# Crossbar transfers of q issued one block sooner in a pooled-attention and MLP kernel

## The chip, the cores and the metric

The kernel runs on one core of one Trainium2 chip. The time is device microseconds of one execution on that core; a lower time is better. Timed runs are given by their median. The profile is one further execution, recorded by the hardware profiler.

## The reference

The inputs q, k and v have the shape 8 batches x 8 heads x 576 rows x 64. Per batch and head, k and v are averaged over groups of 8 rows (72 groups), the scores are taken against the 72 pooled keys, and the softmax of them weighs the 72 pooled values. A residual MLP follows, first over the 576 rows, then over the 512 channels.

```
k_p = k.reshape(B, H, 72, 8, D).mean(axis=3);  v_p likewise
attn = softmax(q @ k_p.T / sqrt(D));  x = (attn @ v_p) -> (B, 576, 512)
u = x + lam * einsum('ts,bsd->btd', w_tok, alpha1 * x + beta1)
out = u + lam * (relu((alpha2 * u + beta2) @ w_ch1) @ w_ch2)     # 512 -> 2048 -> 512
```

All data is float32 in memory; the kernel's matmuls take bf16 and f16.

## The kernel before

The output is cut into 36 chunks of 128 rows, and four chunks make a block, so there are nine blocks n = 0 to 8. Block n runs the channel MLP of its four chunks: 16 steps `mlp_A` (L471; hidden columns, ReLU on ScalarE) and 16 steps `mlp_B` (L487; back to 512 channels, added on VectorE, stored by SP). Woven into it is the attention of batch b = n + 1 and the row mixing that makes the chunks of later blocks. Blocks 7 and 8 have no attention left.

Inside a block the order is written out by hand: a list of pairs (slot, step), sorted by slot (L620 to L648). Slots 0 to 15 hold the 16 steps of `mlp_A`, 16 to 31 those of `mlp_B`; a negative slot comes first in its block. A slot is only a sort key: each engine and each queue takes its own instructions in this order, and waits only for what they need. A step far down the list can therefore run early, on an engine that has nothing in front of it.

The steps that matter here, for one batch b > 1:

- The first 512 rows of q are loaded by GpSimd, two DMAs `q_bf` that turn float32 into bf16 (L79). The raw k and the last 64 rows of q and k (`load_rem`, L91: four DMAs) are loaded by SP, as is v (`load_v`, L101: two DMAs for each half).
- `cast_rem` (L112) casts the last rows of q to bf16 on GpSimd (L116) and sums those of k (L118). `sum_k` (L127) makes the first sums over k on GpSimd (L131, L133).
- `att_F` (L305) turns q so that the head dimension lies on the partitions: a crossbar transfer (DMA transpose) on the SP queue, `qT`, two for a batch (L314). `att_Frem` (its transfer at L332) does the same for the last rows, `rem_qT`, one for a batch. For batches 0 and 1 both go through TensorE.
- `att_K` (from L342) pools k by small matmuls (L348, L351) and VectorE copies the result into `kpT` (L356). `att_V` (from L358) pools v on VectorE. `att_S` multiplies `kpT` with `qT` (L374), then with `rem_qT` (L377), and ScalarE takes the exponential. `att_AV` follows (L393, L397).
- `mix_T` and `mix_uT` make the rows of later blocks; the latter is a crossbar transfer `u_fm` on the SP queue (L456).

In the slots of block n, with b = n + 1 and b > 1: `cast_rem(b)` at -2.0, both `att_F(b)` at -1.1, `sum_k(b)` at -0.9 and 0.3, `att_Frem(b)` at 0.2, `att_V(b)` from 0.2 to 6.2, the v loads of batch b + 1 at 3.5 and 7.5, `att_K(b)` at 4.1 and 6.1, `att_S(b)` from 7.4 on, the stores of the four output chunks at 19, 23, 27 and 31, `mix_uT` from 20.9 on, and the loads of q and k of batch b + 1 at 21.0 and 21.2 with `load_rem(b + 1)` at 21.1. Nothing on GpSimd stands between `sum_k(b)` and those loads of q.

Of the kernel before, what the change touches and what calls it, by code (L numbers as in the profile page):

```python
# [9 lines left out]
BF = mybir.dt.bfloat16  # L10
# [4 lines left out]
P = 128  # L15
# [8 lines left out]
def kernel(  # L24
# [18 lines left out]
    nc = tc.nc  # L43
    ctx.enter_context(tc.manual_schedule())
    B, H, S, D = q.shape

    const = ctx.enter_context(tc.tile_pool(name="const", bufs=1))
    work = ctx.enter_context(tc.tile_pool(name="work", bufs=1))
# [3 lines left out]
    def gp(name):  # L52
        return psA.tile([P, 512], FP, tag="gp", name=name)
# [11 lines left out]
    st1 = {}  # L65

    def new_batch(b):
        st1[b] = {"qT": [None] * 2, "ET": [None] * H, "raw": [None] * 2, "q_raw": [None] * 2, "q": [None] * 2,
                  "k": [None] * 2, "v": [None] * 2}

    def load_qk(b, u, behind=None):

        def rows(src):
            return src[b, 4 * u:4 * u + 4, 0:512, :].rearrange("h (p c) d -> p h (c d)", c=4)

        raw = work.tile([P, 4, 4, D], FP, tag="k_raw", bufs=2, name="k_raw")
        if b > 1:
            bf = work.tile([P, 4, 4, D], BF, tag="q_bf", bufs=4, name="q_bf")
            nc.gpsimd.dma_start(out=bf.rearrange("p h c d -> p h (c d)"), in_=rows(q))  # L79
            st1[b]["q"][u] = bf  # L80
        else:
            q_raw = work.tile([P, 4, 4, D], FP, tag="q_raw", bufs=2, name="q_raw")
            if behind is not None:
                behind.memset(q_raw[:, 0, 0, 0:1], 0.0)
                behind.memset(raw[:, 0, 0, 0:1], 0.0)
            nc.sync.dma_start(out=q_raw.rearrange("p h c d -> p h (c d)"), in_=rows(q))
            st1[b]["q_raw"][u] = q_raw
        nc.sync.dma_start(out=raw.rearrange("p h c d -> p h (c d)"), in_=rows(k))
        st1[b]["raw"][u] = raw

    def load_rem(b, queue=nc.sync):  # L91

        raw = work.tile([P, 2, 2, 2, D], FP, tag="rem_raw", bufs=2, name="rem_raw")
        for i, src in enumerate((q, k)):
            for h in range(2):
                queue.dma_start(
                    out=raw[:, i, h].rearrange("p c d -> p (c d)"),
                    in_=src[b, h::2, 512:576, :].rearrange("a (i c) d -> i a (c d)", c=2))
        st1[b]["rem_raw"] = raw
# [12 lines left out]
    def cast_rem(b, eng, copy=None):  # L112
        raw = st1[b]["rem_raw"]
        rq = work.tile([P, 2, 2, D], BF, tag="rem_q", bufs=2, name="rem_q")
        rk = work.tile([P, 2, 2, D], BF, tag="rem_k", bufs=2, name="rem_k")
        (copy or eng.tensor_copy)(out=rq.rearrange("p c h d -> p h c d"), in_=raw[:, 0])  # L116
        twice = [raw[:, 1, :, c].unsqueeze(2).to_broadcast((P, 2, 2, D)) for c in range(2)]
        eng.tensor_tensor(out=rk, in0=twice[0], in1=twice[1], op=ALU.add)  # L118
        st1[b]["rem"] = rq, rk

    def cast_q(b, u, copy):

        bf = work.tile([P, 4, 4, D], BF, tag="q_bf", bufs=4, name="q_bf")
        copy(out=bf, in_=st1[b]["q_raw"][u])
        st1[b]["q"][u] = bf
# [40 lines left out]
    for i, src in ((1, moe_alpha1), (0, moe_lam)):  # L166
        n = 65 if i in (0, 3) else 1
        nc.gpsimd.dma_start(out=vecs[0:n:64, i],
                            in_=src.unsqueeze(0).to_broadcast((1 + n // 65, DM)))
# [135 lines left out]
    def att_F(b, hp):  # L305


        st = st1[b]
        u, r = hp // 2, hp % 2
        if r == 0:  # L310
            st["qT"][u] = work.tile([P, 8, P], BF, tag="qT", bufs=4, name="qT")
        if b > 1:
            if r == 0:
                nc.sync.dma_start_transpose(out=st["qT"][u],  # L314
                                            in_=st["q"][u].rearrange("p h c d -> p (h c d)"))
            return
        ps_q = gp("ps_q").bitcast(BF)
        for c in range(4):
            nc.tensor.transpose(
                out=ps_q[:, 128 * c:128 * c + 128],  # L320
                in_=st["q"][u][:, 2 * r + c // 2, 2 * (c % 2):2 * (c % 2) + 2].rearrange(
                    "p c d -> p (c d)"),
                identity=identity_bf)
        nc.scalar.copy(out=st["qT"][u][:, 4 * r:4 * r + 4, :],
                       in_=ps_q[:, 0:512].rearrange("p (c t) -> p c t", c=4))

    def att_Frem(b, copy=None):

        st = st1[b]
        st["rem_qT"] = work.tile([P, 2, P], BF, tag="rem_qT", bufs=2, name="rem_qT")  # L330
        if copy is None:
            nc.sync.dma_start_transpose(out=st["rem_qT"],  # L332
                                        in_=st["rem"][0].rearrange("p c h d -> p (c h d)"))
            return
        ps_q = gp("ps_qr").bitcast(BF)
        for c in range(2):
            nc.tensor.transpose(out=ps_q[:, 128 * c:128 * c + 128],
                                in_=st["rem"][0][:, c].rearrange("p h d -> p (h d)"),
                                identity=identity_bf)
        copy(out=st["rem_qT"], in_=ps_q[:, 0:256].rearrange("p (c t) -> p c t", c=2))  # L340
# [244 lines left out]
    def attention(b):  # L585


        late = b == 1
        todo = [(11.9 if late else -2.0, lambda: cast_rem(b, nc.gpsimd)),
                (14.4 if late else 0.2, lambda: att_Frem(b, nc.scalar.copy if late else None))]  # L590
        for u in range(2):
            at = 10.0 + 4.8 * u if late else -1.0 + 1.2 * u
            if late:
                todo.append((at, lambda u=u: cast_q(b, u, nc.gpsimd.tensor_copy)))
            todo.append((at + 0.1, lambda u=u: sum_k(b, u, nc.gpsimd)))
            for r in range(2):
                at = 12.7 + 4.6 * u + 1.6 * r
                hp = 2 * u + r
                todo.append((at if late else -1.1, lambda hp=hp: att_F(b, hp)))
                todo.append((at + 0.5 if late else 0.2 + 2.0 * hp, lambda hp=hp: att_V(b, hp)))  # L600
                if r:
                    todo.append((at + 0.4 if late else 4.1 + 2.0 * u,
                                 lambda u=u: att_K(b, u, nc.vector.tensor_copy)))
        for h in range(8):
            at = 17.0 + 0.9 * h if late else 7.4 + 1.15 * h
            lag = 1.6 if late else 2.0
            todo.append((at, lambda h=h: att_S(b, h)))
            todo.append((at + lag, lambda h=h: att_AV(b, h)))
            if h % 2:
                eng = nc.gpsimd if late and h < 5 else nc.vector  # L610
                todo.append((at + lag + 0.1, lambda h=h, eng=eng: att_X(b, h - 1, h + 1, eng)))
        for c in range(5):
            at = 26.2 + 0.9 * c if late else 19.1 + 1.3 * c
            todo.append((at, lambda c=c: mix_T(b, c)))
            if c < 4 or b % 2:
                key = (b, c) if c < 4 else (b - 1, 4)
                todo.append((at + 1.8, lambda key=key: mix_uT(key)))
        return todo

    for n in range(NBLK):  # L620
        todo = []
        for j in range(0 if n else 4, NJ):
            todo.append((j, lambda j=j: mlp_A(n, j)))
        for m in range(4):
            for part in range(4):
                at = 16 + (4 * m + part if n else 4 * part + m)
                todo.append((at, lambda m=m, part=part: mlp_B(n, m, part)))
        if n == 0:
            todo.append((11.4, lambda: mix_T(0, 4)))
            todo.append((10.8, lambda: (setup_wtok(4, nc.scalar.copy), setup_rowsum(4))))  # L630
            todo.append((13.3, setup_wtok_odd))
            for g in range(1, 4):
                todo.append((4 * g - 0.8, lambda g=g: setup_bias(g)))
            for g in range(4):
                todo.append((4.2 + 1.7 * g, lambda g=g: scale_w2(g)))
        b = n + 1
        if b < B:
            todo += attention(b)
            if b + 1 < B:
                new_batch(b + 1)  # L640
                for u in range(2):
                    at = 20.0 + 0.2 * u if b == 1 else 21.0 + 0.2 * u
                    todo.append((at, lambda b=b, u=u: load_qk(b + 1, u)))
                    at = 22.0 + 0.2 * u if b == 1 else 3.5 + 4.0 * u
                    todo.append((at, lambda b=b, u=u: load_v(b + 1, u)))
                todo.append((20.1 if b == 1 else 21.1, lambda b=b: load_rem(b + 1)))
        for _, do in sorted(todo, key=lambda x: x[0]):
            do()  # L648

# [29 lines left out]
```

## Time and profile before

| | |
|---|---|
| median of 3 runs | 387.51 us (385.63 to 389.5) |
| profiled execution, its time | 388.71 us |
| profiled execution, span from first to last instruction | 387.0 us |
| TensorE (PE) busy | 356.9 us, 92% |
| VectorE (DVE) busy | 229.0 us, 59% |
| ScalarE (ACT) busy | 158.3 us, 41% |
| GpSimd (POOL) busy | 83.4 us, 22% |
| mean granted TensorE clock | 0.976 of 2.4 GHz |

The rows that are quoted further down give the start in us from the first instruction, then the duration in us. PE is TensorE's matmul, PEld its weight load, SPq the queue of SyncE (its rows are the issuing of DMAs, not the transfers). What stands in square brackets is the idle time of the engine ahead of the instruction and what ended it. In the rows by stretch each engine has its busy time with its number of instructions, and behind them come the granted TensorE clock as a share of full speed, the busy share of the DMA engines and the rate they moved.

### The profile page before, as it was taken

What the parts mean: (1) busy time and instruction counts of PE and PEld (TensorE: products, weight loads), DVE (VectorE), ACT (ScalarE), POOL (GpSimd) and SP (SyncE); (2) the same over time, 40 slices, a digit from 0 to 9 for tenths busy, and PEclk for the clock granted to TensorE, in tenths of its full rate; (3) what the DMA queues carried; (4) which work ended last, traced back from release to release, by engine and by line L of the source; (5) the groups of instructions that cost most, each with busy time, mean ns of one, the idle gap of its engine ahead of it and who ended that gap; (6) DMA issues with size and microseconds to landing.
All of it is one profiled execution on the core that took longest, in us unless ns stands there. A gap on an engine that the chain in (4) does not pass through costs nothing.

```text
span 387.0 us, 5796 instructions
## 1 busy us (share of the span) xinstructions
PE 356.9 (92%) x2179; PEld 190.6 (49%) x2179; DVE 229.0 (59%) x459; ACT 158.3 (41%) x317; POOL 83.4 (22%) x94
## 2 busy tenths in 40 slices
PE   2789998799999799979999799969999999999994
PEld 1375655345644464445545454536445644544542
DVE  4796749788775768484776487546748773011011
ACT  2574766127900690067304650348007701722810
POOL 7653143930007000620043002600060000000000
PEclk9999999899999999998999899979999999999999
DMA  8999996656327952895088806792273024002011
GB/s 200 223 192 214 253 219 145 111 102 165 81 79 195 158 109 64 213 168 107 27 219 128 164 2 186 157 165 45 66 208 90 0 56 118 4 29 81 2 52 57
DMA packets 63931, 46.93 MB, mean 121 GB/s; under 512 B 31448, under 2 KB 54044, under 8 KB 63904
## 3 DMA queue, kind: packets, MB, share of 16 engines
q1 hardware_dynamic: 54496, 38.55, 41.8%
q0 software_dynamic: 9408, 8.02, 14.1%
q8 instruction: 17, 0.28, 0.3%
q14 instruction: 10, 0.08, 0.1%
HBM read 38.04 MB, written 9.44 MB: 123 GB/s over the span
## 4 chain that ended last, share of the span: by engine, by line
PE 80%; DMA 11%; DVE 4%; issue 1%; ACT 1%; SPq 1%; POOL 1%; POOLq 0%; DVEq 0%
PE ps_ch L495 30%; PE ps_h L477 29%; PE ps_tok L442 11%; PE ps_sc L374 4%; DMA rem_qT<-rem_q 3%; DMA v_u<-in_v_dram 3%; DMA rem_raw<-in_q_dram 3%; PE ps_av L393 2%; DMA vecs<-in_moe_beta_dram 2%; PE ps_sc L377 1%; DVE xs L408 1%; DVE v_u L362 1%; PE ps_w L247 1%; DVE x_tm L401 1%; PE ps_bc L229 1%
## 5 line engine op out<-in xcount | busy, mean ns | idle before, releaser
L482 ACT ACTIVATE Hj<-ps_h,bias_cols 128x512 bf16<-128x512 f32 x144 | 98.5, 688 | 161.5 <-PE ps_h L477 160.5
L477 PE MATMUL ps_h<-u_fm,w 128*128 128x512 bf16 (+2 forms) x592 | 141.9, 383 | 0.0
L495 PE MATMUL ps_ch<-w,Hj 128*128 128x512 bf16 x576 | 135.3, 380 | 0.0
L477 PEld LDWEIGHTS <-w 128*128 128x128 bf16 x592 | 63.2, 115 | 51.4 <-issue 8.0
L495 PEld LDWEIGHTS <-Hj 128*128 128x128 bf16 x576 | 55.3, 98 | 62.4 <-issue 1.1
L500 DVE TENSOR_TENSOR u_sb<-u_sb,ps_ch 128x512 f32<-128x512 f32 x36 | 24.7, 687 | 73.0 <-PE ps_ch L495 72.6
L442 PE MATMUL ps_tok<-xs,wtT 128*128 128x512 bf16 (+1 forms) x200 | 50.8, 387 | 2.7 <-DVE xs L408 2.7
L379 ACT ACTIVATE ET<-ps_sc 72x256 f16<-72x256 f32 (+1 forms) x128 | 45.0, 403 | 14.0 <-PE ps_sc L374 9.0
L444 DVE TENSOR_TENSOR u_sb<-x_tm,ps_tok 128x512 f32<-128x512 f32 (+1 forms) x40 | 27.5, 687 | 25.6 <-PE ps_tok L442 24.0
L116 POOL CAST rem_q<-rem_raw 128x256 bf16<-128x256 f32 x7 | 4.5, 646 | 167.9 <-DMA rem_raw<-in_q_dram 167.8
L362 DVE TENSOR_TENSOR v_u<-v_u 72x512 f32<-72x512 f32 x64 | 37.3, 583 | 2.0 <-DMA v_u<-in_v_dram 0.4
L374 PE MATMUL ps_sc<-qT,kpT 128*72 128x256 bf16 x128 | 27.6, 300 | 8.9 <-DMA qT<-q_bf 4.5
L401 DVE TENSOR_TENSOR x_tm<-ps_av,rec 128x320 f32<-128x320 f32 x64 | 31.4, 491 | 2.3
L442 PEld LDWEIGHTS <-wtT 128*128 128x128 bf16 (+1 forms) x200 | 19.4, 99 | 26.4 <-issue 5.0
L399 DVE RECIPROCAL rec<-ps_av 128x5 f32<-128x5 f32 x64 | 12.2, 191 | 31.7 <-PE ps_av L397 30.8
L446 DVE TENSOR_TENSOR u_bf<-u_sb,al_bc 128x512 bf16<-128x512 f32 (+1 forms) x38 | 29.3, 771 | 1.5
L393 PEld LDWEIGHTS <-ET 72*128 72x128 f16 x256 | 16.7, 102 | 12.6 <-ACT ET L379 1.0
L408 DVE TENSOR_TENSOR xs<-x_tm,lamal_bc 128x512 bf16<-128x512 f32 x29 | 22.0, 758 | 0.9
L131 POOL TENSOR_TENSOR k_raw<-k_raw 128x512 f32<-128x512 f32 x16 | 21.2, 1326 | 4.9 <-DMA k_raw<-in_k_dram 4.9
L133 POOL TENSOR_TENSOR k_bf<-k_raw 128x512 bf16<-128x512 f32 x16 | 21.7, 1358 | 1.3
L374 PEld LDWEIGHTS <-kpT 128*72 128x72 bf16 x128 | 12.5, 123 | 15.7 <-DVE v_u L362 4.8
L393 PE MATMUL ps_av<-vp,ET 72*128 72x66 f16 x256 | 18.7, 200 | 0.4 <-ACT ET L379 0.4
(98 smaller groups left out, 208.8 us busy)
## 6 DMA issues: line engine op xcount, KB each, us to landing
k_raw<-in_k_dram SPq DMA_DIRECT2D x16, 512.0 KB
v_u<-in_v_dram SPq DMA_DIRECT2D x16, 512.0 KB
out_dram<-u_sb SPq DMA_DIRECT2D x32, 256.0 KB
w<-in_moe_w_ch_dram POOLq DMA_DIRECT2D x8, 512.0 KB, 14.1
q_bf<-in_q_dram POOLq DMA_DIRECT2D x12, 256.0 KB, 5.7
q_raw<-in_q_dram SPq DMA_DIRECT2D x4, 512.0 KB
rem_raw<-in_q_dram SPq DMA_DIRECT2D x16, 64.0 KB
rem_raw<-in_k_dram SPq DMA_DIRECT2D x16, 64.0 KB
```

The lines of the kernel that those rows point to most:

```text
L362: nc.vector.tensor_tensor(out=t[:, :, 0:n], in0=t[:, :, 0:n], in1=t[:, :, n:2 * n], op=ALU.add)
L374: nc.tensor.matmul(out=ps_sc[0:SPG, 0:256], lhsT=kpT_pool[u][:, half, h % 4, :], rhs=st["qT"][u][:, 2 * (h % 4):2 * (h % 4) + 2, :])
L379: nc.scalar.activation(out=ET[:, n0:n0 + n], in_=ps_sc[0:SPG, 0:n], func=AF.Exp, bias=0.0, scale=0.125)
L393: nc.tensor.matmul(out=av[:, c, :], lhsT=ET[:, m0:m0 + 128], rhs=vp1[:, hh, :])
L401: nc.vector.tensor_tensor(out=x[:, :, dd:dd + D], in0=av[:, :, 0:64], in1=rec.unsqueeze(2).to_broadcast((P, 5, D)), op=ALU.mult)
L408: eng.tensor_tensor(out=xs[:, 0:4, cols], in0=x[:, 0:4, cols], in1=lamal_bc[:, cols].unsqueeze(1).to_broadcast((P, 4, D * (h1 - h0))), op= ...
L442: nc.tensor.matmul(out=ps_tok, lhsT=wtT[0:kk, at, t0:t0 + P], rhs=xs[0:kk, sc, :], start=(sc == 0), stop=(sc == 4))
L444: nc.vector.tensor_tensor(out=s["u"][p0:p1, :], in0=st1[b]["x"][p0:p1, c, :], in1=ps_tok[p0:p1, 0:DM], op=ALU.add)
L446: eng.tensor_tensor(out=s["u_bf"][p0:p1, :], in0=s["u"][p0:p1, :], in1=al2_bc[p0:p1, :], op=ALU.mult)
L477: nc.tensor.matmul(out=ps_h[:, t0:t1], lhsT=w1_of(cc, j), rhs=u_fm[n][:, cc, t0:t1], start=(cc == 0), stop=(cc == 3))
L482: nc.scalar.activation(out=t, in_=ps_h, func=AF.Relu, bias=bias_cols[:, j:j + 1], scale=1.0)
L495: nc.tensor.matmul(out=ps, lhsT=Hj[n, j][:, 128 * m:128 * m + 128], rhs=w2[j // 4][:, j % 4, :], start=(j == 0), stop=(j == NJ - 1))
```

## The change

For batches 3 to 7 the two transfers `qT` move from slot -1.1 of the block that uses them to slots 10.0 and 10.1 of the block before, and `cast_rem` with `att_Frem` from -2.0 and 0.2 to 27.4 and 27.5 of the block before. The loads `q_bf` of the next batch become a step of their own, at slots 0.4 and 0.5 in place of 21.0 and 21.2, and `load_rem` goes from 21.1 to 20.9, which sorts it ahead of the first `mix_uT` (19.1 + 1.8 is just above 20.9 in floating point). Batch 2 keeps the old places of its transfers; its q loads stay in block 0. Nothing is computed in another way.

```diff
--- before.py
+++ after.py
@@ -68,24 +68,26 @@
         st1[b] = {"qT": [None] * 2, "ET": [None] * H, "raw": [None] * 2, "q_raw": [None] * 2, "q": [None] * 2,
                   "k": [None] * 2, "v": [None] * 2}
 
+    def rows(src, b, u):
+        return src[b, 4 * u:4 * u + 4, 0:512, :].rearrange("h (p c) d -> p h (c d)", c=4)
+
+    def load_q_bf(b, u):
+
+        bf = work.tile([P, 4, 4, D], BF, tag="q_bf", bufs=4, name="q_bf")
+        nc.gpsimd.dma_start(out=bf.rearrange("p h c d -> p h (c d)"), in_=rows(q, b, u))
+        st1[b]["q"][u] = bf
+
     def load_qk(b, u, behind=None):
 
-        def rows(src):
-            return src[b, 4 * u:4 * u + 4, 0:512, :].rearrange("h (p c) d -> p h (c d)", c=4)
-
         raw = work.tile([P, 4, 4, D], FP, tag="k_raw", bufs=2, name="k_raw")
-        if b > 1:
-            bf = work.tile([P, 4, 4, D], BF, tag="q_bf", bufs=4, name="q_bf")
-            nc.gpsimd.dma_start(out=bf.rearrange("p h c d -> p h (c d)"), in_=rows(q))
-            st1[b]["q"][u] = bf
-        else:
+        if b < 2:
             q_raw = work.tile([P, 4, 4, D], FP, tag="q_raw", bufs=2, name="q_raw")
             if behind is not None:
                 behind.memset(q_raw[:, 0, 0, 0:1], 0.0)
                 behind.memset(raw[:, 0, 0, 0:1], 0.0)
-            nc.sync.dma_start(out=q_raw.rearrange("p h c d -> p h (c d)"), in_=rows(q))
+            nc.sync.dma_start(out=q_raw.rearrange("p h c d -> p h (c d)"), in_=rows(q, b, u))
             st1[b]["q_raw"][u] = q_raw
-        nc.sync.dma_start(out=raw.rearrange("p h c d -> p h (c d)"), in_=rows(k))
+        nc.sync.dma_start(out=raw.rearrange("p h c d -> p h (c d)"), in_=rows(k, b, u))
         st1[b]["raw"][u] = raw
 
     def load_rem(b, queue=nc.sync):
@@ -586,8 +588,17 @@
 
 
         late = b == 1
-        todo = [(11.9 if late else -2.0, lambda: cast_rem(b, nc.gpsimd)),
-                (14.4 if late else 0.2, lambda: att_Frem(b, nc.scalar.copy if late else None))]
+        todo = []
+        if late:
+            todo = [(11.9, lambda: cast_rem(b, nc.gpsimd)),
+                    (14.4, lambda: att_Frem(b, nc.scalar.copy))]
+        if b == 2:
+            todo = [(-2.0, lambda: cast_rem(b, nc.gpsimd)), (0.2, lambda: att_Frem(b))]
+        if 1 < b < B - 1:
+            todo.append((10.0, lambda: att_F(b + 1, 0)))
+            todo.append((10.1, lambda: att_F(b + 1, 2)))
+            todo.append((27.4, lambda: cast_rem(b + 1, nc.gpsimd)))
+            todo.append((27.5, lambda: att_Frem(b + 1)))
         for u in range(2):
             at = 10.0 + 4.8 * u if late else -1.0 + 1.2 * u
             if late:
@@ -596,7 +607,8 @@
             for r in range(2):
                 at = 12.7 + 4.6 * u + 1.6 * r
                 hp = 2 * u + r
-                todo.append((at if late else -1.1, lambda hp=hp: att_F(b, hp)))
+                if b < 3:
+                    todo.append((at if late else -1.1, lambda hp=hp: att_F(b, hp)))
                 todo.append((at + 0.5 if late else 0.2 + 2.0 * hp, lambda hp=hp: att_V(b, hp)))
                 if r:
                     todo.append((at + 0.4 if late else 4.1 + 2.0 * u,
@@ -641,9 +653,11 @@
                 for u in range(2):
                     at = 20.0 + 0.2 * u if b == 1 else 21.0 + 0.2 * u
                     todo.append((at, lambda b=b, u=u: load_qk(b + 1, u)))
+                    todo.append((at if b == 1 else 0.4 + 0.1 * u,
+                                 lambda b=b, u=u: load_q_bf(b + 1, u)))
                     at = 22.0 + 0.2 * u if b == 1 else 3.5 + 4.0 * u
                     todo.append((at, lambda b=b, u=u: load_v(b + 1, u)))
-                todo.append((20.1 if b == 1 else 21.1, lambda b=b: load_rem(b + 1)))
+                todo.append((20.1 if b == 1 else 20.9, lambda b=b: load_rem(b + 1)))
         for _, do in sorted(todo, key=lambda x: x[0]):
             do()
 
```

## Rows read from the trace of the kernel before

**Rows 1.** Page, chain that ended last: shares of the span by line.

```profile
PE ps_ch L495 30%; PE ps_h L477 29%; PE ps_tok L442 11%; PE ps_sc L374 4%; DMA rem_qT<-rem_q 3%; DMA v_u<-in_v_dram 3%; DMA rem_raw<-in_q_dram 3%; PE ps_av L393 2%; DMA vecs<-in_moe_beta_dram 2%; PE ps_sc L377 1%; DVE xs L408 1%; DVE v_u L362 1%; PE ps_w L247 1%; DVE x_tm L401 1%; PE ps_bc L229 1%
```

**Rows 2.** Busy time by stretch, one row for each of blocks 1 to 6.

```profile
87.94:124.99 37.05, 37.05 (x230) 19.81 (x229) 26.43 (x54) 15.98 (x33) 6.82 (x7) 1.00 0.55 134
124.99:164.34 39.35, 37.38 (x230) 19.73 (x229) 26.50 (x54) 15.73 (x32) 7.64 (x8) 1.00 0.63 132
164.34:205.69 41.35, 38.80 (x231) 20.08 (x229) 26.52 (x54) 15.84 (x32) 9.24 (x10) 0.96 0.61 130
205.69:246.54 40.85, 38.90 (x230) 20.13 (x229) 26.99 (x54) 15.84 (x32) 8.24 (x9) 0.96 0.61 128
246.54:289.70 43.16, 39.95 (x231) 20.52 (x229) 25.78 (x54) 15.84 (x32) 7.53 (x8) 0.92 0.61 123
289.70:326.76 37.06, 37.06 (x231) 19.82 (x229) 26.21 (x54) 15.40 (x32) 0.49 (x1) 1.00 0.26 63
```

**Rows 3.** Waits of the whole span at the scores: us in total, times, longest.

```profile
PE ps_sc L374 <- DMA qT<-q_bf: 4.5, 3, 2.0
...
PE ps_sc L377 <- DMA rem_qT<-rem_q: 3.3, 4, 1.2
...
PE ps_sc L374 <- DVE v_u L362: 1.9, 1, 1.9
```

**Rows 4.** TensorE in order of time: blocks 5 and 6.

```profile
252.60 0.28 PE L348 MATMUL ps_kp<-pool_main,k_bf 128*128 128x64 bf16 x4
...
255.76 0.38 PE L374 MATMUL ps_sc<-qT,kpT 128*72 128x256 bf16 x2 [1.96 <-DMA qT<-q_bf]
257.39 0.24 PE L377 MATMUL ps_sc<-rem_qT,kpT 128*72 128x64 bf16 x1 [1.25 <-DMA rem_qT<-rem_q]
...
296.80 0.38 PE L374 MATMUL ps_sc<-qT,kpT 128*72 128x256 bf16 x2
```

**Rows 5.** Busy time by stretch, the 10 us around block 5's first scores.

```profile
253.80:263.80 10.00, 6.79 (x35) 3.58 (x35) 2.74 (x8) 4.25 (x10) 0.00 (x0) 0.66 0.92 166
```

**Rows 6.** SP queue in order of time: starts of blocks 1, 3, 5, 6.

```profile
89.00 2.75 SPq L314 DMA_TRANSPOSE qT<-q_bf  x2
...
165.52 4.44 SPq L314 DMA_TRANSPOSE qT<-q_bf  x2
...
245.06 2.60 SPq L502 DMA_DIRECT2D out_dram<-u_sb  x2
247.77 5.99 SPq L314 DMA_TRANSPOSE qT<-q_bf  x2
254.23 1.17 SPq L332 DMA_TRANSPOSE rem_qT<-rem_q  x1
255.50 2.55 SPq L108 DMA_DIRECT2D v_u<-in_v_dram  x4
274.68 0.37 SPq L502 DMA_DIRECT2D out_dram<-u_sb  x1
...
290.88 2.66 SPq L314 DMA_TRANSPOSE qT<-q_bf  x2
```

**Rows 7.** GpSimd in order of time, around the start of block 5.

```profile
239.50 0.76 POOL L116 CAST rem_q<-rem_raw 128x256 bf16<-128x256 f32 x1 [32.45 <-DMA rem_raw<-in_q_dram]
...
245.16 1.26 POOL L133 TENSOR_TENSOR k_bf<-k_raw 128x512 bf16<-128x512 f32 x1
246.37 1.53 POOL L79 DMA_DIRECT2D q_bf<-in_q_dram  x2
```

**Rows 8.** The instructions of tile q_bf: its loads, issue to landing.

```profile
DMA to landing us min/median/max: 4.3/5.7/7.9
```

**Rows 9.** Chain of waits in order of time, block 3.

```profile
170.07 4.43 DMA rem_qT<-rem_q
```

**Rows 10.** VectorE in order of time: blocks 3 and 5.

```profile
168.86 0.94 DVE L356 CAST kpT<-ps_kp 64x288 bf16<-64x288 f32 x2 [1.03 <-PE ps_kp L351]
...
255.64 0.29 DVE L364 TENSOR_TENSOR vp<-v_u 72x128 f16<-72x128 f32 x1
```

## The prediction

> **What bounds the kernel now.** I read first the chain that ended last. Three TensorE lines, the two MLP halves and the row mixing, hold 70% of the span; two of the DMA entries, at 3% each, are transfers for q's last rows, `rem_qT` and the load of their raw data [rows 1]. So TensorE sets the end and the question is where it stands still or runs slowly.
>
> The busy time by block answers that. Blocks 1 to 6 have the same TensorE work, 230 or 231 matmuls each, but blocks 1 and 6 take 37.05 and 37.06 us with TensorE busy all the time at full clock, while blocks 2 to 5 take 39.35, 41.35, 40.85 and 43.16 us [rows 2]. Over 37.05 that is 2.30 + 4.30 + 3.80 + 6.11 = 16.51 us. It has two parts. TensorE is idle for span less busy time: 1.97 + 2.55 + 1.95 + 3.21 = 9.68 us. And its busy time is longer than 37.05 by 0.33 + 1.75 + 1.85 + 2.90 = 6.83 us, with a mean granted clock of 0.96, 0.96 and 0.92 in blocks 3 to 5 and 1.00 in block 2 [rows 2].
>
> The waits name the idle part: 4.5 us on `qT` in three blocks, 3.3 us on `rem_qT` in four, and 1.9 us once put down to VectorE: 9.7 us in all, the whole 9.68 [rows 3]. Block 5 shows the place: TensorE idles 1.96 us ahead of the first scores until `qT` lands and 1.25 us more until `rem_qT` lands, while in block 6 the same scores start 7.10 us after the block's start with no wait [rows 4]. The 10 us around block 5's stall have a granted clock of 0.66 [rows 5], a mix of the levels 1.2 and 2.4 GHz: the clock fell after the idle time, and the matmuls behind it ran slowly. So the second part comes out of the first.
>
> The 1.9 us belong to `qT` too, as I read it. It is block 3's wait, where the first scores need `kpT`'s first half; VectorE had that ready at 168.86 + 0.94 = 169.80 [rows 10], and block 3's `rem_qT` transfer, which SP issues behind both `qT`, ran from 170.07 for 4.43 us [rows 9], to 174.50, well after the scores could have begun at 164.34 + 7.10 = 171.44.
>
> Why is `qT` late? On the SP queue both transfers stand behind the previous block's last stores. In block 5 they start at 247.77, 1.2 us into the block, and SP needs 5.99 us to issue the two; block 3's pair takes 4.44. In blocks 1 and 6 the same two take 2.75 and 2.66 us [rows 6]. What differs is GpSimd: in block 5 it issues both q loads of the next batch at 246.37, just as SP comes to the transfers [rows 7]; block 6 has no next batch, and block 1's loads were issued in block 0. Those loads take 4.3 to 7.9 us to land [rows 8].
>
> **The change, part by part.** All times are those of block 5, the worst one, unless said.
>
> *The two `qT`* leave the block's start. Removed from the path: the first wait of each of blocks 2 to 5, 4.5 + 1.9 = 6.4 us [rows 3]. Their new place is behind the v loads of the block before. SP ends those at 255.50 + 2.55 = 258.05 and next has something to do at 274.68 [rows 6], 16.6 us later, or 10.5 us once the block is 6.11 us shorter. The loads they need were issued by 246.37 + 1.53 = 247.90 and land within 7.9 us [rows 7, 8], at 255.8, so SP doesn't stand there for them. No row shows `qT` behind v loads; I bound it by the rows with and without a load beside it, 2.66 and 5.99 us, and take 5.99, since v is then still in flight. Either end fits into the 10.5 us, and the result is needed most of a block later: cost 0. Without that cover each further us would push the store at slot 19 and then the loads of k.
>
> *`cast_rem` and `att_Frem`* leave the block's start as well: removed, the four second waits, 3.3 us [rows 3]. In time the cast hardly moves: it already ran at 239.50, as soon as its data came, 32.45 us after GpSimd had nothing else to do [rows 7]. On SP the transfer now stands between the stores of chunks 2 and 3; the first of these two began at 245.06 and one store takes 0.37 to issue [rows 6], so it goes out at about 245.5. The same transfer at 254.23 released TensorE at 257.39, 3.16 us later [rows 4, 6], and block 3's took 4.43 [rows 9]. By the longer it lands at 250, and a TensorE without stalls wants it at about 246.54 + 7.10 + 0.2 = 253.8. Cost 0, cover 3.8 us. Its issue of 1.17 us [rows 6] delays only the store of chunk 3 and the v loads, which nobody waits for within the block.
>
> *The q loads* go from slot 21 to 0.4, but GpSimd already issues them when `k_bf` ends, at 246.37 against 245.16 + 1.26 = 246.42 [rows 7]; nothing of its own stood between. Same place, cost 0.
>
> *`load_rem`* goes ahead of the first `mix_uT` and the k loads. Four issues like it take SP 2.55 us (the v loads, rows 6), so the first k load may come up to 2.55 us later; the second stands behind the same work as before. The k sums ended at 246.42 and the second half's are first used at 252.60 [rows 4, 7]: 6.2 us of cover. Cost 0.
>
> *The clock.* With the stalls gone nothing is left that slows it: in blocks 1 and 6, which have no stall, it is 1.00 throughout [rows 2]. The bounds of what goes: 9.7 us, if only the waits went, and 16.5 us, if these blocks become like 1 and 6. I take 16.5, because those two blocks have the same matmuls and the same VectorE chain, and differ in just this point. More can't be gained: a block without idle time at full clock is 37.05 us.
>
> The sum is 388.71 - 16.51 = 372.2 us for the profiled execution. That execution is 1.20 us above the median of 387.51, so against the median I say **371.0 us**.
>
> **Rivals.**
>
> *A. The last rows stay late.* `att_Frem` meets the loads again: it goes out at about 245.5 and GpSimd's loads at 246.37 [rows 7], while k sums that end earlier would bring those loads forward too. If its transfer then takes over twice the 4.43 us, the 3.3 us of second waits [rows 3] remain, with none to all of the 6.83 us of slow matmuls: 374.3 to 381.1. For it speaks that `qT` took twice as long beside these loads [rows 6]; against it, that the transfer alone, beside the same loads, never took over 4.43. The Trainium skill (DMA: Bandwidth & Descriptors, section on queues, rings and completion order) says that each DMA engine goes round between the queues that have work, a packet of each at a time. By that rule being issued ahead of the loads buys only the head start and no precedence, which is this rival; the trace agrees so far as the slower `qT` show it.
>
> *B. The same wait under another name.* If block 3's 1.9 us really were VectorE's, and the k and v chain on VectorE were as late as `qT` in all four blocks, the scores would start no sooner: 386 to 388. Against it: `kpT` was ready at 169.80, and block 6 has that chain and starts on time [rows 4, 10].
>
> *C. Slower: SP is held at slot 10.* `qT` now stands ahead of the stores, of `mix_uT` and of the loads of k on an in-order queue. Should the two transfers hold SP for long, the k loads come late and TensorE waits at the k matmuls of the next block (252.60 in block 5). It takes 10.5 us to use up SP's idle time and 6.2 us more to use up the k sums' cover. From 16.7 us on each us costs one in each of blocks 2 to 6, and from 20 us on the 16.5 us gained are lost; at 21 us it is 371.0 + 5 x 4.3 = 392.5. The longest pair so far took 5.99.
>
> **How the numbers follow.** About 1% is what a measurement of this kernel can tell from no change: the three runs lie within 0.5% of their median. Forecast 0.74; A 0.14; B 0.08; C 0.04. The forecast spreads by the runs' own 2 us downwards, to 369, and upwards to the lower bound of the gain, 387.5 - 9.7 = 377.8. The range 369 to 378 holds nearly all of the forecast and the cheaper half of A, near 0.8. Faster by over 1% (under 383.6): the forecast and A, 0.88. Within 1%: B, 0.08. Slower: C, 0.04.
>
> **What the changed profile would show.** Right: blocks 2 to 5 at 37 to 38 us each with a clock of 1.00, no wait at the first scores, `rem_qT` gone from the chain, the pairs of `qT` on SP about 11 us into the block before, and SP idle again before the first store. A would show as waits on `rem_qT` of 0.6 us and more in the scores; B as waits of the scores on VectorE; C as waits of the k matmuls on GpSimd. Wrong above all would be any block among 2 to 5 that still takes 39 us, or blocks without idle time that are longer than 37.05 us.

## The result and the profile after

The changed kernel takes 372.22 us (median of 4 runs, 370.7 to 372.95) against 387.85 us before (4 runs): a ratio of 0.9595, 95% interval 0.9538 to 0.9653. The forecast was 371.0, range 369 to 378. The profiled execution takes 372.95 us with a span of 371.2 us; 372.2 was forecast for it.

The busy time by block (blocks 1 to 6, columns as in [rows 2]; some matmul records are missing, 225 to 227 of 230 are there):

```profile
88.70:125.73 37.03, 36.76 (x225) 19.81 (x229) 26.38 (x54) 15.98 (x33) 6.63 (x7) 1.00 0.64 150
125.73:162.80 37.07, 36.86 (x227) 19.83 (x229) 26.21 (x54) 15.40 (x32) 7.28 (x8) 1.00 0.68 143
162.80:199.85 37.05, 36.84 (x226) 19.80 (x229) 26.18 (x54) 15.40 (x32) 9.60 (x11) 1.00 0.71 143
199.85:236.90 37.05, 36.78 (x225) 19.83 (x229) 26.45 (x54) 15.40 (x32) 8.02 (x8) 1.00 0.66 144
236.90:273.95 37.05, 36.84 (x226) 19.81 (x229) 26.16 (x54) 15.40 (x32) 7.34 (x8) 1.00 0.68 141
273.95:311.00 37.05, 36.78 (x225) 19.79 (x229) 26.22 (x54) 15.40 (x32) 0.00 (x0) 1.00 0.18 47
```

All six blocks are 37.03 to 37.07 us with the clock at 1.00. Blocks 2 to 5 fall from 164.71 us [rows 2] to 148.22 us: 16.49 us, where 16.51 was forecast. The span fell by 15.8 us; the difference lies ahead of block 1, which starts at 88.70 here and at 87.94 before. No instruction of that stretch was changed, and the starts of block 1 in this and the experiments' profiles are spread from 85.3 to 88.7. In this profile and in that of before the granted clock is 0.50 (1.2 GHz) for some of block 0, at 77 to 79 us here and at 76 to 78 before; in the second and the third experiment's, where block 1 starts at 85.3 and 85.9, it stays at 1.00 from 60 us on.

The scores of block 5 on TensorE, which answer to [rows 4]:

```profile
244.00 0.38 PE L376 MATMUL ps_sc<-qT,kpT 128*72 128x256 bf16 x2
244.22 0.24 PE L379 MATMUL ps_sc<-rem_qT,kpT 128*72 128x64 bf16 x1
```

They start 7.10 us into the block, as in block 6 before, and wait for nothing. The SP queue of block 5 and GpSimd around it, which answer to [rows 6, 7]:

```profile
234.72 1.19 SPq L334 DMA_TRANSPOSE rem_qT<-rem_q  x1
...
240.41 7.11 SPq L110 DMA_DIRECT2D v_u<-in_v_dram  x4
247.62 4.07 SPq L316 DMA_TRANSPOSE qT<-q_bf  x2
258.91 0.37 SPq L504 DMA_DIRECT2D out_dram<-u_sb  x1
...
271.69 1.19 SPq L334 DMA_TRANSPOSE rem_qT<-rem_q  x1
```

```profile
236.18 1.53 POOL L77 DMA_DIRECT2D q_bf<-in_q_dram  x2
...
267.56 1.26 POOL L133 TENSOR_TENSOR k_raw<-k_raw 128x512 f32<-128x512 f32 x1 [3.05 <-DMA k_raw<-in_k_dram]
...
271.80 1.27 POOL L135 TENSOR_TENSOR k_bf<-k_raw 128x512 bf16<-128x512 f32 x1
```

The pair `qT` now goes out 10.7 us into the block before its use, takes 4.07 us and is done 7.2 us before SP's next store. `rem_qT` goes out 2.2 us ahead of block 5 and 1.5 us ahead of GpSimd's loads; over blocks 2 to 5 it is 1.2 to 2.3 us ahead of the block and 1.3 to 2.0 us ahead of the loads. GpSimd issues these loads at the block's start, as ever.

### The profile page after: what moved, and what is told of

Same layout as the page of the kernel before. It is cut to its first block, busy times and chain, and to the rows that moved or that the text cites. A ratio compares the mean times of both kernels' runs of the same rounds, so it can differ in the third digit from the quotient of the medians.

```text
span 371.2 us, 5743 instructions
## 1 busy us (share of the span) xinstructions
PE 347.1 (93%) x2139; PEld 188.5 (51%) x2179; DVE 226.5 (61%) x459; ACT 156.7 (42%) x317; POOL 83.0 (22%) x94
## 4 chain that ended last, share of the span: by engine, by line
PE 80%; DMA 8%; DVE 8%; issue 2%; POOL 1%; SPq 0%; POOLq 0%; DVEq 0%
PE ps_ch L497 32%; PE ps_h L479 30%; PE ps_tok L444 11%; DMA v_u<-in_v_dram 3%; PE ps_sc L376 3%; DMA rem_raw<-in_q_dram 3%; DVE v_u L364 2%; DMA vecs<-in_moe_beta_dram 2%; PE ps_av L395 2%; DVE x_tm L403 2%; DVE xs L410 1%; PE ps_sc L379 1%; DVE vp L366 1%; DVE rec L401 1%; DVE xs L519 0%
## 5 line engine op out<-in xcount | busy, mean ns | idle before, releaser
L479 PE MATMUL ps_h<-u_fm,w 128*128 128x512 bf16 (+2 forms) x571 | 136.1, 374 | 1.1
L444 PE MATMUL ps_tok<-xs,wtT 128*128 128x512 bf16 (+1 forms) x195 | 49.7, 384 | 3.7 <-DVE xs L410 3.5
L446 DVE TENSOR_TENSOR u_sb<-x_tm,ps_tok 128x512 f32<-128x512 f32 (+1 forms) x40 | 27.5, 688 | 24.8 <-PE ps_tok L444 24.2
L364 DVE TENSOR_TENSOR v_u<-v_u 72x512 f32<-72x512 f32 x64 | 36.3, 567 | 4.8 <-DMA v_u<-in_v_dram 3.3
L118 POOL CAST rem_q<-rem_raw 128x256 bf16<-128x256 f32 x7 | 3.0, 429 | 132.2 <-DMA rem_raw<-in_q_dram 132.2
L376 PE MATMUL ps_sc<-qT,kpT 128*72 128x256 bf16 x128 | 26.7, 291 | 3.1 <-DVE x_tm L403 1.8
L395 PEld LDWEIGHTS <-ET 72*128 72x128 f16 x256 | 16.5, 102 | 12.2 <-DVE v_u L364 0.8
L358 DVE CAST kpT<-ps_kp 64x288 bf16<-64x288 f32 x28 | 12.7, 455 | 7.7 <-PE ps_kp L353 7.3
```

Source lines behind the costliest of these rows:

```text
L364: nc.vector.tensor_tensor(out=t[:, :, 0:n], in0=t[:, :, 0:n], in1=t[:, :, n:2 * n], op=ALU.add)
L376: nc.tensor.matmul(out=ps_sc[0:SPG, 0:256], lhsT=kpT_pool[u][:, half, h % 4, :], rhs=st["qT"][u][:, 2 * (h % 4):2 * (h % 4) + 2, :])
L395: nc.tensor.matmul(out=av[:, c, :], lhsT=ET[:, m0:m0 + 128], rhs=vp1[:, hh, :])
L444: nc.tensor.matmul(out=ps_tok, lhsT=wtT[0:kk, at, t0:t0 + P], rhs=xs[0:kk, sc, :], start=(sc == 0), stop=(sc == 4))
L446: nc.vector.tensor_tensor(out=s["u"][p0:p1, :], in0=st1[b]["x"][p0:p1, c, :], in1=ps_tok[p0:p1, 0:DM], op=ALU.add)
L479: nc.tensor.matmul(out=ps_h[:, t0:t1], lhsT=w1_of(cc, j), rhs=u_fm[n][:, cc, t0:t1], start=(cc == 0), stop=(cc == 3))
```

## The experiments

The theory to test was that TensorE waits because SP needs 4.4 to 6 us for a pair of `qT` beside GpSimd's q loads. Its rivals: the last rows are late on their own account; or the place behind the last stores makes `qT` late, whatever runs beside it.

**Only the two `qT` moved.**

```diff
-        if b == 2:
+        if b >= 2:
             todo = [(-2.0, lambda: cast_rem(b, nc.gpsimd)), (0.2, lambda: att_Frem(b))]
...
-            todo.append((27.4, lambda: cast_rem(b + 1, nc.gpsimd)))
-            todo.append((27.5, lambda: att_Frem(b + 1)))
```

> The change with the cast and the transfer of q's last rows put back to slots -2.0 and 0.2; only the two qT stay moved. Theory (the stalls come from SP taking 4.4 to 6 us for the two qT beside GpSimd's q loads): with them gone SP reaches rem_qT some 1.2 us into the block instead of 6 to 8, it lands by 6 us, TensorE wants it 7.3 us in: no wait, 372 to 373 us, the whole gain. Rival (the last rows are late on their own account, beside the q loads): waits of 0.6 us and more on rem_qT stay in blocks 2 to 5, with slow matmuls behind them: 375 to 380 us.

Measured: 374.12 us, ratio 0.9651 (0.9564 to 0.9738). Four of blocks 1 to 5 take 37.05 to 37.10 us, block 3 takes 38.41. Its busy time, its rows on TensorE, GpSimd's loads, and its chain of waits:

```profile
161.87:200.28 38.41, 37.20 (x230) 19.80 (x229) 26.04 (x54) 15.62 (x32) 9.26 (x11) 1.00 0.69 137
```

```profile
168.97 0.38 PE L376 MATMUL ps_sc<-qT,kpT 128*72 128x256 bf16 x2
170.56 0.24 PE L379 MATMUL ps_sc<-rem_qT,kpT 128*72 128x64 bf16 x1 [1.21 <-DMA rem_qT<-rem_q]
```

```profile
162.01 1.54 POOL L77 DMA_DIRECT2D q_bf<-in_q_dram  x2
```

```profile
163.06 7.46 DMA rem_qT<-rem_q
```

The theory holds in three of the four blocks; in one the last rows' transfer, issued 1.05 us after the loads, took 7.46 us beside them, where it had 6.1 (out 1.2 us into the block, wanted at 7.3). So the two `qT` bring nearly all of the gain (block 3 loses 1.36 us, and the intervals of this ratio and of the change's overlap), and the rival is right about one block.

**Only the last rows moved.**

```diff
-            todo.append((10.0, lambda: att_F(b + 1, 0)))
-            todo.append((10.1, lambda: att_F(b + 1, 2)))
...
-                if b < 3:
+                if True:
                     todo.append((at if late else -1.1, lambda hp=hp: att_F(b, hp)))
```

> The change with the two qT put back to slot -1.1 of the block that uses them; only the cast and the transfer of the last rows stay moved. Theory: the waits on qT stay, 6.4 us in blocks 2 to 5, those on rem_qT (3.3 us) go, and of the 6.8 us of slow matmuls some part goes with the shorter idle time: 379 to 386 us. Rival (the last transfer alone is what TensorE ends up waiting for): 372 to 375 us.

Measured: 375.75 us, ratio 0.9707 (0.9624 to 0.979), between the two expectations: the theory's 379 us was too high. The blocks 2 to 5, and the waits at the scores:

```profile
122.35:160.63 38.28, 37.21 (x230) 19.75 (x229) 26.20 (x54) 15.62 (x32) 7.14 (x8) 1.00 0.65 137
160.63:199.30 38.67, 37.21 (x231) 19.72 (x229) 25.75 (x54) 15.62 (x32) 9.82 (x11) 1.00 0.70 137
199.30:236.37 37.07, 37.07 (x231) 19.82 (x229) 26.75 (x54) 15.40 (x32) 7.94 (x9) 1.00 0.62 144
236.37:275.38 39.01, 37.20 (x230) 19.72 (x229) 26.10 (x54) 15.62 (x32) 7.18 (x7) 1.00 0.64 134
```

```profile
PE ps_sc L376 <- DVE v_u L364: 3.3, 2, 1.8
PE ps_sc L376 <- DMA qT<-q_bf: 1.1, 1, 1.1
```

They lose 4.8 us together over 37.05, in place of 16.5. The waits ahead of the scores come to 4.4 us, not 6.4, and none on `rem_qT` is left; the pair still takes SP 4.5 to 6.2 us. The profile puts 3.3 us of these waits, in blocks 3 and 5, down to VectorE, as it did with block 3's before; the next experiment tells which it is. The clock stays at 1.00, and the busy time over 37.05 falls from 6.83 to 0.49 us, where I had expected more of it to stay. That is the fastest of the four executions, 374.36 us; the slowest took 378.93 at a mean clock of 0.989, so it need not hold in each. GpSimd's loads came 0.9 us ahead of blocks 4 and 5, where it was 0.2 us before, and 0.2 us ahead of block 2 in both. Block 4's wait is gone, block 5's only fell from 1.96 to 1.81 us: why the waits got shorter is not shown.

**The kernel before, with the loads somewhere else.** They leave `load_qk` and become a step of their own; shown in part.

```diff
+    def load_q_bf(b, u, behind=None):
+        bf = work.tile([P, 4, 4, D], BF, tag="q_bf", bufs=4, name="q_bf")
+        if behind is not None:
+            behind.memset(bf[:, 0, 0, 0:1], 0.0)
+        nc.gpsimd.dma_start(...)
...
+                    todo.append((at if b < 3 else 9.0 + 0.1 * u,
+                                 lambda b=b, u=u: load_q_bf(b + 1, u, None if b < 3 else nc.vector)))
```

> The kernel before, all transfers at their old places; only GpSimd's q loads of batches 4 to 7 are held behind a small VectorE write at slot 9, so that they run some 10 us into the block instead of at its start. Theory (the loads beside the transfers are the cause): SP issues each pair of qT in 2.7 to 2.9 us as in blocks 1 and 6, the scores don't wait, blocks 2 to 5 take 37 to 37.5 us: 371 to 374 us. Rival (the place of the transfers behind the last stores is the cause): the pair still ends too late, 384 to 389 us.

Measured: 371.84 us, ratio 0.959 (0.9519 to 0.966), as good as the change. The blocks 2 to 5, its SP queue at the starts of blocks 4 and 5, and GpSimd's loads in block 4:

```profile
122.98:160.04 37.06, 37.06 (x231) 19.82 (x229) 26.22 (x56) 15.40 (x32) 7.12 (x8) 1.00 0.69 142
160.04:197.08 37.04, 37.04 (x231) 19.82 (x229) 26.89 (x56) 15.40 (x32) 9.59 (x9) 1.00 0.64 143
197.08:234.14 37.06, 37.06 (x231) 19.82 (x229) 27.01 (x56) 15.40 (x32) 8.23 (x8) 1.00 0.68 141
234.14:271.18 37.04, 37.04 (x231) 19.82 (x229) 26.54 (x56) 15.40 (x32) 8.31 (x8) 1.00 0.68 144
```

```profile
198.26 2.65 SPq L319 DMA_TRANSPOSE qT<-q_bf  x2
201.01 1.19 SPq L337 DMA_TRANSPOSE rem_qT<-rem_q  x1
...
235.37 3.27 SPq L319 DMA_TRANSPOSE qT<-q_bf  x2
```

```profile
206.80 1.53 POOL L76 DMA_DIRECT2D q_bf<-in_q_dram  x2 [9.83 <-DVE q_bf L75]
```

The pairs of blocks 2 to 5 take 2.65 to 3.27 us, all blocks 37.04 to 37.06. Here every transfer stands where it stood before, behind the last stores. That settles the cause: the loads beside the transfers, and not their place behind the stores. VectorE's chain is no later or earlier than before: in block 3 it starts on `kpT` 4.52 us into the block in both kernels (168.86 in [rows 10], block from 164.34), and yet the scores start 7.11 us into it without a wait:

```profile
164.56 0.94 DVE L361 CAST kpT<-ps_kp 64x288 bf16<-64x288 f32 x2 [0.68 <-PE ps_kp L356]
```

```profile
167.15 0.38 PE L379 MATMUL ps_sc<-qT,kpT 128*72 128x256 bf16 x2
```

So the waits that the profiles put down to VectorE were waits for `qT`.

**Idle time filled.** The kernel before with matmuls of no use in the gap.

```diff
+        if 2 < b < 7:
+            todo.append((7.3, lambda: keep_warm(8)))
```

> The kernel before with 8 extra matmuls (128x512, result unused) ahead of the first scores of blocks 2 to 5, 8 x 0.216 = 1.73 us of work in place of idle time; the transfers are as late as before. Theory (the clock falls because TensorE stood idle): idle time per block falls from 2.0 to 3.2 us to 0.5 to 1.5 us, the clock stays at 1.00, the 6.8 us of slow matmuls go, and where the wait was under 1.73 us some 0.4 us is added: 380 to 383 us. Rival (the clock falls for another reason): the slow matmuls stay, 387 to 390 us, or up to 395 us if the extra matmuls come on top.

Measured: 382.86 us, ratio 0.9885 (0.9813 to 0.9956), as expected. Blocks 2 to 5:

```profile
124.34:163.90 39.56, 38.96 (x239) 20.57 (x237) 27.16 (x54) 15.73 (x32) 7.88 (x9) 1.00 0.64 130
163.90:203.82 39.92, 39.09 (x238) 20.51 (x237) 26.59 (x54) 15.73 (x32) 8.57 (x10) 1.00 0.64 136
203.82:243.09 39.27, 38.95 (x239) 20.63 (x237) 26.98 (x54) 15.73 (x32) 8.07 (x9) 1.00 0.63 129
243.09:283.59 40.50, 39.09 (x238) 20.53 (x237) 26.52 (x54) 15.73 (x32) 8.13 (x8) 1.00 0.62 135
```

Busy time over 37.05 is 7.89 us, of which the 32 extra matmuls are 6.91 (at 0.216), so 0.98 us is left in place of 6.83, and the clock is 1.00; the idle time fell from 9.68 to 3.16 us. The transfers were as late as before (5.6 to 6.2 us for a pair). So the slow clock came from the idle time; work of no use in its place made the kernel 1.2% faster.

**SP held on purpose** (rival C of the prediction), by loads that land late ahead of the pair; shown for the first run, the second has 18.8 and 18.95.

```diff
     def load_q_bf(b, u, behind=None):
...
+        if behind is not None:
+            behind.memset(bf[:, 0, 0, 0:1], 0.0)
...
-            todo.append((10.0, lambda: att_F(b + 1, 0)))
+            todo.append((14.65, lambda: att_F(b + 1, 0)))
...
-                    todo.append((at if b == 1 else 0.4 + 0.1 * u,
+                    todo.append((at if b == 1 else 14.5 + 0.1 * u,
```

> The changed kernel with its q loads held behind a small VectorE write at slot 14.5 and both qT at slot 14.65, ahead of the store at slot 19: SP has to stand still until the loads have landed. In the changed kernel's block 5 SP comes to that store 22 us into the block. Loads issued at 17 to 18.6 us, 4.3 to 7.9 us to land, 2.7 to 4.8 us for the pair: SP comes free at 25.6 to 31.3 us, 3.6 to 9.3 us late. Theory (cover of 6.9 us by the k sums, the tightest thing behind SP): nothing up to 2.4 us lost in each of blocks 2 to 6, at the k matmuls: 372 to 384 us. Rival (the u_fm transfers have less cover, some 3 us, and only at the starts of blocks 2 and 3): 1 to 12 us lost, at the first MLP matmuls of these two blocks alone: 373 to 385 us, with blocks 4 to 6 at 37.05.

> As the run before with the loads held to slot 18.8 and the pair at 18.95: SP comes free at 30.3 to 36 us, 8.3 to 14 us late. Theory (k sums with 6.9 us of cover): 1.4 to 7.1 us lost in each of blocks 2 to 6, at the k matmuls: 379 to 408 us. Rival (u_fm alone, starts of blocks 2 and 3): 382 to 394 us, with blocks 4 to 6 at 37.05.

Measured: 372.31 us, ratio 0.9563 (0.9504 to 0.9622), and 395.95 us, ratio 1.0196 (1.0119 to 1.0274). The hold of SP is counted here from the end of its v loads to the end of the pair. In block 5 of the first run it is 246.22 to 260.92, 14.7 us, and block 6 starts on time, after 37.04 us:

```profile
239.23 6.99 SPq L112 DMA_DIRECT2D v_u<-in_v_dram  x4
257.15 3.77 SPq L318 DMA_TRANSPOSE qT<-q_bf  x2
```

In blocks 1 to 4 it is 13.3 to 13.8 us, and only block 2 is longer, by 0.3 us (37.35), with no wait that the profile names. SP came free 25.3 us into block 5, below the 25.6 to 31.3 expected, so this run decides nothing between theory and rival.

In block 3 of the second run the hold is 184.75 to 202.85, 18.1 us, and that kernel is some 2% slower than before. Its SP queue, its first MLP matmuls of blocks 3 and 4, and TensorE's waits from block 1 on:

```profile
175.32 9.43 SPq L112 DMA_DIRECT2D v_u<-in_v_dram  x4
200.00 2.85 SPq L318 DMA_TRANSPOSE qT<-q_bf  x2
202.95 0.53 SPq L506 DMA_DIRECT2D out_dram<-u_sb  x1
```

```profile
171.78 0.59 PE L481 MATMUL ps_h<-u_fm,w 128*128 128x512 bf16 x1 [4.96 <-DMA u_fm<-u_bf]
...
213.78 6.17 PE L481 MATMUL ps_h<-u_fm,w 128*128 128x512 bf16 x20 [2.57 <-DMA u_fm<-u_bf]
```

```profile
PE ps_h L481 <- DMA u_fm<-u_bf: 14.3, 4, 5.0
PE ps_sc L378 <- DVE kpT L360: 1.1, 1, 1.1
PE ps_kp L352 <- POOL k_bf L137: 0.6, 1, 0.6
```

The wait is on `u_fm`, at the starts of blocks 2 to 5 (4.08, 4.96, 2.57 and 2.72 us); the k matmuls wait 0.6 us once, in block 6. So the theory of both expectations, that the k sums are the tightest thing behind SP, fell. The rival named the right transfer, but not the right blocks: it has four, not two.

No experiment points beyond the two kernels at 372 us: the change and the run with the loads elsewhere both reach 37.05 us, within 0.02, in blocks 1 to 6, where the profile shows no wait of TensorE's matmuls.

## Why the prediction was right

**The stalls of blocks 2 to 5.** Right in place and size: 16.49 us against 16.51. That block 3's 1.9 us, which the profile puts down to VectorE, belong to `qT`, against rival B, is shown by the loads-elsewhere run, where VectorE's chain is as before and that wait is gone.

**Why `qT` was late.** I named two things, the stores ahead of it and the loads beside it, and said that the loads make the difference. The third run shows it alone. The two halves don't add up either: each by itself gives 11 to 14 us of the 15.6 (3.5% and 2.9% of 388). In the first run three of the four waits on `rem_qT` went with the `qT`; in the second, 6.3 us of the busy time over 37.05 went with the 5.3 us of waits, in the execution that was profiled.

**`qT` behind the v loads.** Bounded by 2.66 and 5.99 us, taken at 5.99; measured 3.88 to 4.84 in five blocks (4.07 in block 5). Cost 0 was right.

**`rem_qT`.** Forecast to go out about 1 us ahead of its block with 3.8 us of cover; measured 1.2 to 2.3 us ahead, without a wait. The argument against rival A was wrong, though: I said that this transfer, beside the same loads, never took over 4.43 us, and in the first run it took 7.46. The transfers of before were hardly beside the loads:

```profile
131.91 2.65 DMA rem_qT<-rem_q
```

```profile
212.46 2.78 DMA rem_qT<-rem_q
```

```profile
254.23 3.13 DMA rem_qT<-rem_q
```

In blocks 2, 4 and 5 they went out 7 to 8 us after GpSimd began to issue the loads, which had all landed within 0.9 us of that: in block 5 the second load was issued at 247.2 and took 7.9 us at most [rows 8], to 255.1; in blocks 2 and 4 they were issued at 125.6 and 206.3 and took 7.0. In block 3 the second was issued at 165.8 and took 7.4 us at most, so up to 3.1 us of it were still to come at 170.07: there the transfer took the 4.43. In the changed kernel the transfer goes out 1.3 to 2.0 us ahead of the loads and no wait is left; how long it took there the profile does not show. From 1.2 us ahead of the block even 7.46 us would land 6.3 us into it, ahead of the scores' 7.3. So by these profiles moving the last rows, once the `qT` are moved, is worth 1.4 us at times and otherwise nothing.

**q loads and `load_rem`.** The loads stayed at the block's start, 0.7 us ahead of block 5 (0.2 us before). GpSimd now waits 3.05 us for k where it had not waited, since `load_rem` goes first, but its k sums end at 273.07, 0.9 us ahead of block 6: cost 0.

**The clock.** The 6.83 us were taken to follow from the idle time, and the run with filled gaps shows that for all but 0.98 us, which is there at a clock of 1.00.

**Rival C.** The mechanism exists, but the step that priced it was wrong: I let the k sums decide, with the first us lost at 16.7 us of hold. By that 18.1 us would have cost 7 us in five blocks; it cost 24, of which 16 are waits and the rest slow matmuls. The transfers `u_fm`, which I had named there without a deadline of their own, have less cover. The holds of blocks 1 to 4 were 17.9, 18.4, 18.1 and 18.2 us; less the wait behind each, the first us is lost at 13.4 to 15.5 us, an estimate that fits the first run, which lost 0.3 us at 13.3 in block 2 and nothing in the others. Behind block 5's 18.3 us no wait on `u_fm` followed. Since the changed kernel holds SP for some 4 us, this touches neither sum nor sign.

## What to carry to other kernels

Before moving a late transfer, ask what else moves at the same moment: here the same 16 us were to be had by moving either the transfer or the load beside it, and the busy time of SP for the same pair (2.7 us in two blocks, 4.4 to 6 in four) told so in the profile of before. Count a stall of TensorE with what the clock takes afterwards: 9.7 us of waits cost 16.5. And when a step is put ahead of others on an in-order queue, list every transfer behind it with its own deadline; the one to which I gave none was the tightest.

## What was not expected of the hardware

The transfer of the last rows, 128 x 256 bf16, took 2.65 to 3.13 us where the loads were all but done, and 7.46 us where it went out 1.05 us after them. And the granted clock does not follow from the amount of idle time alone: before, block 2 had 1.97 us of it and kept 1.00, block 4 had 1.95 us and fell to 0.96 [rows 2]; with only the last rows moved, block 5 had 1.81 us and kept 1.00.
